# Far tokens of a fused transformer block transposed by VectorE from 32-blocks, and six weight sums issued in the MLP

## The chip, the cores and the metric

The kernel runs on one core of a Trainium2 chip. The metric is the device time of one execution in microseconds (us): 1777.04, the median of 3 runs (1775.67 to 1777.31). A core has TensorE (PE in the profile; PEld is its weight load), VectorE (DVE), ScalarE (ACT), GpSimd (POOL) and SyncE (SP, which here issues nearly all DMAs). Each engine takes its own instructions in the order in which the program lists them, and waits on semaphores where it needs another's result.

## The reference

All in float32: x is 2048 x 1024, wqkv 1024 x 3072, 32 heads of 32 features, an MLP of width 3584.

```python
qkv = layernorm(x) @ wqkv                       # split into q, k, v by head
pq, pk = (per head: q @ w_phi, k @ w_phi)
phi_q = [softmax(pq), softmax(-pq)];  phi_k = [softmax(pk), softmax(-pk)]
kv = einsum("hsf,hsd->hfd", phi_k, v);  z = sum over s of phi_k
o = (phi_q @ kv) / (phi_q . z + 1e-6)
h = x + o @ wo
out = h + relu(layernorm(h) @ w1) @ w2
```

## The kernel before

The 2048 tokens are 16 tiles of 128: tiles 0 to 7 are the near half, 8 to 15 the far half. Every product is done with both operands split into a high part (rounded to the fast format fp32r) and a low part (the rest), as three matmuls: high x high, high x low, low x high. A weight unit of 128 x 512 is loaded into a "raw" tile (6 of them), ACT makes the high part (L126), VectorE or GpSimd the low part (L131), into a ring of ten "w" tiles; the raw tile is then free for the next load.

Stages, in PE's order: for the near half the keys and values (four slabs s of 256 columns, one item for each tile and slab), then the queries (two slabs); the same for the far half; then the attention output and wo; then the MLP: 98 up items for each half of the tokens, and the down items. The MLP's two products are done in the manner of Strassen with seven products in place of eight, so it reads, beside blocks of w1 and w2, sums of blocks. These 56 weight sums are made ahead of time: `t_load` brings four blocks of 128 x 256 into one tile, `t_sum` subtracts four times on GpSimd (L401), `t_store` writes the tile to a scratch tensor t. `sums_at` says at which step each one stands: 45 before and in the attention stage, 11 in the MLP. In the MLP the tile is y2 (name "y" in the trace), with one buffer, so a load waits for the store before it.

The order of everything beside the matmuls is written out by hand. `when(step, f, ...)` hangs f on a step; a step is three large matmuls of PE. An item of the attention stage has 8 steps, an up item of the MLP 4. `up0` is the first step of the MLP. `W.advance` puts the loads and splits of weights between the steps, as the rings come free.

A tile of x is loaded (`ln_load`, L239), its mean and variance taken (`ln_stats`, `ln_power`, which leaves scale and bias), normalized by ACT (`ln_norm`, L262), transposed by PE in two groups of four (`ln_turn`, L281) into a PSUM bank "tp" (2 of them), from where ACT takes the high part (L180) and VectorE the low part (L181) into xT. xT has eight buffers, so far tile t can be written only when PE is done with near tile t - 8, in the second query slab. The statistics of the far tiles are taken much earlier, from a load of its own ("s", steps 80 to 214), and kept in scx; the far tile is loaded a second time. The far half's hidden states later go another way (`far_pair`): loaded so that VectorE's 32 x 32 transposes suffice, with scales spread over the partitions by `far_scale` (16 small matmuls, L833, and one ACT copy).

A chunk k of xT holds 128 features; before, features 128k to 128k + 127. The key and query weights are multiplied by w_phi beforehand ("folded"): slab 0 at the very start by `fold_mm` (L315), the others by `fold_all` (L326) at seven steps up to 232.

```python
turn = 8 * n + 1                                     # n: the item after near tile t - 8's last
load_ = turn - 88 + 8 * (t - HT) if t < HT + 4 else turn - 36
stages = (load_, None, None, turn - 8, turn + 1, turn + 1)
```

For the second half of the tokens in the MLP, its transposed states hT are loaded (L885, fourteen loads of 512 KB) at steps up0 + 344 to up0 + 407, each when the first half's last product of that kind is done, split by ACT (L893) and VectorE (L897), and read from step up0 + 392 on.

Of the kernel before, what the change touches and what calls it, by code (L numbers as in the profile page):

```python
# [46 lines left out]
UP = (1, 5, 6, 2, 7, 3, 4)  # L47
DOWN = (1, 5, 6, 3, 7, 2, 4)
OPENS = (1, 5, 2)
FOLD_STEPS = 31, 76, 104, 144, 176, 206, 232  # L50
BANK_OF = {6: 1, 7: 1, 4: 1, 3: 5}

# [90 lines left out]
def kernel(  # L143
# [31 lines left out]
    def f32(ap):  # L175
        return ap.bitcast(F32)
# [57 lines left out]
    def ln_load(key, parts):  # L234
        xin[key] = xlp.tile([P, D], F32, name="xl") if key[0] == "x" and key[1] >= HT and key[1] % 4 > 1 else \
            lnp.tile([P, D], F32, name="xin")
        n = D // len(parts)
        for j, p in enumerate(parts):
            sp.dma_start(xin[key][:, j * n:(j + 1) * n], p)  # L239
# [17 lines left out]
        xst[key] = sc  # L257

    def ln_norm(key):
        sc, src = xst.pop(("s", key[1]) if key[0] == "x" and key[1] >= HT else key), xin.pop(key)  # L260
        xnt[key] = src if key[0] == "h" else fp_ln.tile([P, D], F32, name="xn")
        act.activation(xnt[key], src, AF.Identity, bias=sc[:, 1:2], scale=sc[:, 0:1])  # L262

    def ln_norm_by(key, engines):

        sc, src = xst.pop(key), xin.pop(key)
        xnt[key] = xn = fp_ln.tile([P, D], F32, name="xn")
        n = D // len(engines)
        for j, eng in enumerate(engines):
            cols = slice(j * n, (j + 1) * n)  # L270
            if eng is act:
                act.activation(xn[:, cols], src[:, cols], AF.Identity, bias=sc[:, 1:2], scale=sc[:, 0:1])
            else:
                eng.tensor_scalar(xn[:, cols], src[:, cols], sc[:, 0:1], sc[:, 1:2], op0=ALU.mult, op1=ALU.add)

    def ln_turn(key, j, dst=None):

# [33 lines left out]
            wt_of[p, i] = t  # L311

    def fold_mm(k, ps, i):
        if True:
            pe.matmul(ps[:, i * P:(i + 1) * P], wt_of[0, i][:, k * P:(k + 1) * P],  # L315
                      bd[:, i, :], start=True, stop=True)

    def fold_all(p):

        banks = [(ac_bank if p == 1 else tp_bank)() for _ in range(2)] + [mm_bank() for _ in range(2)]  # L320
        for i in range(2):
            wt = wt_of.pop((p, i)).rearrange("p (c q d) -> p c q d", q=4, d=32)
            for r in range(4):
                rows = slice(32 * r, 32 * (r + 1))
                for q in range(4):
                    pe.matmul(banks[r][32 * q:32 * (q + 1), 256 * i:256 * (i + 1)],  # L326
                              wphi[rows, (2 * p + i) % 8, :], wt[rows, :, q, :], start=True, stop=True)
        fold_ps[p] = banks
# [26 lines left out]
    def load(key, t):  # L355

        kind = key[0]
        if kind == "kv":
            _, hf, s, k = key
            sp.dma_start(t[:, 0:256], wpk[s][k])  # L360
            sp.dma_start(t[:, 256:512], wv[s, k])
        elif kind == "q":
            _, _, s, k = key
            sp.dma_start(t, wpq[s][k])
        elif kind == "wo":
            _, hf, c = key
            sp.dma_start(t, wo[hf, c])
        elif kind == "a":
            sp.dma_start(t, ad[key[1:]])
        else:  # L370
            _, _, m, p = key
            w = 1 if kind == "w1" else 2
            sp.dma_start(t, block(w, p, *{1: (0, 0), 2: (1, 0), 3: (1, 1)}[m]) if m < 4
                         else td[w, p][:, {5: 0, 7: 3 - w, 4: w, 6: 3}[m], :])

    def block(w, p, r, c):

# [30 lines left out]
    def first_values():  # L408

        for k in range(0, NK, 2):  # L410
            if k == 4:
                ln_load(("x", 1), x_part(1))
            place = W.raws.take()
            t = place[1]
            sp.dma_start(t.rearrange("p (k f) -> p k f", k=2), wv[0, k:k + 2].rearrange("k p f -> p k f"))
            for i in range(2):
                first_raw[k + i] = t[:, 256 * i:256 * (i + 1)], place
        W.loaded = W.done = NK

# [407 lines left out]
    hst = {}  # L827

    def far_scale():
        ps = tp_bank()[:, 0:64].rearrange("p (g n s) -> p g n s", g=4, n=HT)  # L830
        for g in range(4):
            for a in range(4):
                pe.matmul(ps[32 * a:32 * (a + 1), g], ident.rearrange("p (t g) -> p g t", g=4)[:, g],  # L833
                          scx[:, :, 0, :], start=True, stop=True)
        act.activation(scx.rearrange("p n g s -> p g n s"), ps, AF.Copy)

# [236 lines left out]
    def when(step, f, *args):  # L1073
# [3 lines left out]
        else:  # L1077
# [200 lines left out]
    for b in range(2):  # L1278
# [7 lines left out]

    sixth, fourth = (10, 19, 28, 37, 46, 55), (10, 19, 28, 37)
    sums_at = [30, 39, 47] + [64 * i + k for i in (1, 2, 3) for k in sixth] + \
        [266, 276, 286, 296, 332, 342, 352, 362, 372] + \
        [64 * i + k for i, places in ((6, fourth), (7, fourth), (8, fourth), (9, (14, 26, 38))) for k in places] + \  # L1290
        [up0 + 424 + 30 * i for i in range(11)]
    for n, (w, p, j) in enumerate((w, p, j) for w in (1, 2) for p in range(NP) for j in range(2)):
        step = sums_at[n]
        half_on = sums_at.index(64 * 6 + 10)
# [122 lines left out]
```

## Time and profile before

| what | value |
|---|---|
| median of 3 runs | 1777.04 us |
| the profiled execution, whole | 1776.94 us |
| its span, first to last instruction | 1774.9 us |
| HBM traffic | 295.31 MB read, 137.89 MB written, 244 GB/s over the span |
| sums on GpSimd, tiles b, y, xn | 121.2, 38.4 and 22.5 us busy |

The span is cut into 40 slices on the page; a digit is the busy share in tenths:

```profile
DVE  7888778777789878664656664454434333343333
ACT  5322245333333342455555654444444444444442
POOL 4788745878847998432433344434354454544443
DMA  7899788655476777987889988787787777877775
```

A slice is 44.4 us. The far tiles stand in slices 5 and 6 (222 to 311 us), the MLP from slice 17 on. A group row of the profile names line, engine, operation, tiles and count, then "busy us, mean ns of one", then idle time of the engine before it and what ended that. A row of waits reads "who waited <- for whom: us in total, times, longest".

### The profile page before, as it was taken

What the parts mean: (1) busy time and instruction counts of PE and PEld (TensorE: products, weight loads), DVE (VectorE), ACT (ScalarE), POOL (GpSimd) and SP (SyncE); (2) the same over time, 40 slices, a digit from 0 to 9 for tenths busy, and PEclk for the clock granted to TensorE, in tenths of its full rate; (3) what the DMA queues carried; (4) which work ended last, traced back from release to release, by engine and by line L of the source; (5) the groups of instructions that cost most, each with busy time, mean ns of one, the idle gap of its engine ahead of it and who ended that gap; (6) DMA issues with size and microseconds to landing.
All of it is one profiled execution on the core that took longest, in us unless ns stands there. A gap on an engine that the chain in (4) does not pass through costs nothing.

```text
span 1774.9 us, 28930 instructions
## 1 busy us (share of the span) xinstructions
PE 1767.2 (100%) x10088; PEld 1528.4 (86%) x10088; DVE 1078.5 (61%) x1650; ACT 766.9 (43%) x1378; POOL 978.8 (55%) x990
## 2 busy tenths in 40 slices
PE   9999999999999999999999999999999999999999
PEld 8888888888888888888888888888888888888887
DVE  7888778777789878664656664454434333343333
ACT  5322245333333342455555654444444444444442
POOL 4788745878847998432433344434354454544443
PEclk9999999999999999999999999999999999999999
DMA  7899788655476777987889988787787777877775
GB/s 224 270 312 314 256 274 278 196 174 166 144 214 215 244 251 226 304 271 227 254 267 281 367 289 259 252 272 255 231 247 222 230 230 240 260 226 228 228 227 183
DMA packets 335234, 435.13 MB, mean 245 GB/s; under 512 B 29296, under 2 KB 195184, under 8 KB 335088
## 3 DMA queue, kind: packets, MB, share of 16 engines
q1 hardware_dynamic: 301008, 415.98, 73.8%
q10 hardware_dynamic: 34080, 17.31, 3.4%
q8 instruction: 79, 1.29, 0.3%
q14 instruction: 67, 0.55, 0.1%
HBM read 295.31 MB, written 137.89 MB: 244 GB/s over the span
## 4 chain that ended last, share of the span: by engine, by line
PE 92%; DVE 3%; DMA 2%; POOL 2%; issue 1%; ACT 0%; SPq 0%; ACTq 0%; DVEq 0%; POOLq 0%
PE mm L205 22%; PE mm L206 22%; PE mm L207 22%; PE ac L206 4%; PE ac L205 4%; PE ac L207 4%; PE tp L207 2%; PE tp L206 2%; PE tp L205 2%; PE mm L200 1%; PE mm L197 1%; PE mm L196 1%; PE tp L281 1%; PE ac L503 1%; POOL w L131 1%
## 5 line engine op out<-in xcount | busy, mean ns | idle before, releaser
L131 POOL TENSOR_TENSOR w<-raw,w 128x512 fp32r<-128x512 f32 x356 | 472.9, 1330 | 606.7 <-ACT w L126 582.6
L126 ACT ACTIVATE w<-raw 128x512 fp32r<-128x512 f32 x686 | 410.2, 625 | 482.7 <-PE mm L207 221.3
L131 DVE TENSOR_TENSOR w<-raw,w 128x512 fp32r<-128x512 f32 x330 | 273.7, 831 | 467.5 <-ACT w L126 461.5
L205 PE MATMUL mm<-w,xT 128*128 128x512 f32 x680 | 262.6, 386 | 0.0
L206 PE MATMUL mm<-w,xT 128*128 128x512 f32 x680 | 258.3, 380 | 0.4 <-POOL sc L254 0.4
L207 PE MATMUL mm<-w,xT 128*128 128x512 f32 x680 | 258.0, 379 | 0.0
L207 PE MATMUL mm<-hT,w 128*128 128x512 f32 x624 | 236.7, 379 | 0.0
L205 PE MATMUL mm<-hT,w 128*128 128x512 f32 x624 | 236.7, 379 | 0.0
L206 PE MATMUL mm<-hT,w 128*128 128x512 f32 x624 | 236.7, 379 | 0.0
L207 PE MATMUL mm<-w 128*128 128x512 f32 x392 | 148.7, 379 | 0.0
L205 PE MATMUL mm<-w 128*128 128x512 f32 x392 | 148.7, 379 | 0.0
L206 PE MATMUL mm<-w 128*128 128x512 f32 x392 | 148.7, 379 | 0.0
L205 PEld LDWEIGHTS mm<-w,xT 128*128 128x128 f32 x680 | 128.7, 189 | 22.2 <-issue 4.1
L401 POOL TENSOR_TENSOR b<-b 128x256 f32<-128x256 f32 x152 | 121.2, 797 | 47.7 <-DMA b<-in_w_dram 40.3
L206 PEld LDWEIGHTS mm<-w,xT 128*128 128x128 f32 x680 | 128.8, 189 | 18.4 <-POOL sc L254 0.9
L207 PEld LDWEIGHTS mm<-w,xT 128*128 128x128 f32 x680 | 128.8, 189 | 18.1 <-DVE xT L181 0.2
L206 PEld LDWEIGHTS mm<-hT,w 128*128 128x128 f32 x624 | 118.2, 189 | 16.6
L205 PEld LDWEIGHTS mm<-hT,w 128*128 128x128 f32 x624 | 118.2, 189 | 16.5
L207 PEld LDWEIGHTS mm<-hT,w 128*128 128x128 f32 x624 | 118.2, 189 | 16.5
L492 POOL TENSOR_TENSOR zacc<-zacc,kphi 128x512 f32<-128x512 f32 x60 | 79.2, 1320 | 16.0 <-DVE kphi L484 15.4
L476 ACT ACTIVATE ke<-ke 128x512 f32<-128x512 f32 x64 | 40.3, 630 | 100.9 <-DVE ke L472 100.8
L207 PEld LDWEIGHTS mm<-w 128*128 128x128 f32 x392 | 74.2, 189 | 10.4
(194 smaller groups left out, 3366.1 us busy)
## 6 DMA issues: line engine op xcount, KB each, us to landing
raw<-t SPq DMA_DIRECT2D x224, 256.0 KB, 4.1
raw<-ad SPq DMA_DIRECT2D x196, 256.0 KB, 3.1
raw<-in_w_dram SPq DMA_DIRECT2D x168, 256.0 KB, 3.5
ad<-c SPq DMA_DIRECT2D x112, 256.0 KB, 4.5
ad<-s SPq DMA_DIRECT2D x84, 256.0 KB, 4.7
b<-in_w_dram SPq DMA_DIRECT2D x38, 512.0 KB, 5.6
t<-b SPq DMA_DIRECT2D x38, 512.0 KB, 4.8
ed<-qe ACTq DMA_DIRECT2D x64, 256.0 KB, 3.7
```

Source lines behind the costliest of these rows:

```text
L126: nc.scalar.activation(w[:, 0, :], raw[1], AF.Copy)
L131: eng.tensor_tensor(out=w[:, 1, :], in0=raw[1], in1=w[:, 0, :].bitcast(F32), op=ALU.subtract)
L196: pe.matmul(ps, a_hi, woven(b_hi), start=first and k == 0, stop=False, skip_group_check=more)
L197: pe.matmul(ps, a_lo, woven(b_hi), start=False, stop=False, skip_group_check=more)
L200: pe.matmul(ps, a_hi, woven(b_lo), start=False, stop=last and j == n - 1, skip_group_check=more)
L205: pe.matmul(ps, a_hi, b_hi, start=first, stop=False, skip_group_check=more)
L206: pe.matmul(ps, a_hi, b_lo, start=False, stop=False, skip_group_check=more)
L207: pe.matmul(ps, a_lo, b_hi, start=False, stop=last, skip_group_check=more)
L281: pe.transpose(pt[:, k, :], xn[:, (4 * j + k) * P:(4 * j + k + 1) * P], ident)
L401: pool.tensor_tensor(out=tsum[*u, *out], in0=tsum[*u, *a], in1=tsum[*u, *b], op=ALU.subtract)
L476: act.activation(e_of[key], e_of[key], AF.Exp)
L492: pool.tensor_tensor(out=zacc[s], in0=zacc[s], in1=phi_of[key], op=ALU.add)
```

## The change

1. *Far tiles.* `ln_load` reads a far tile in four DMAs of 32 tokens: partition 32a + t holds token 32g + t's features 256a to 256a + 255, g by columns. Each partition has thus four tokens, so `x_scale` (step 226) spreads the scales as `far_scale` does. `x_norm` normalizes in place with four ACT instructions of 256 columns, `x_turn` transposes all 32 x 32 blocks with one VectorE instruction, `x_high` makes the high part on ACT, `x_low` the low part on GpSimd in two instructions. Tile t's transpose stands at step 334 + 11(t - 8), its load 26 steps ahead, its low part 6 steps behind.
2. *Features.* The blocks come out with four groups of 32 features in a chunk: chunk k holds features 256a + 32k + i. All that meets xT follows: near tiles are normalized into that order (`chunked`, `dst_order`), value rows are read in it (`value_rows`), and both folds take their columns in it. `fold_mm` becomes four matmuls with 32 output rows in place of one with 128; the first value loads are eight DMAs in place of four.
3. *Sums.* Five sums at steps 332 to 372 and one of four around 394 to 421 leave the attention stage. The MLP has 17 in place of 11, every 23 steps from up0 + 360 in place of every 30 from up0 + 424; their loads stand 12 steps ahead of the sum in place of 15.

```diff
+        if key[0] == "x" and key[1] >= HT:
+            for g in range(4):
+                sp.dma_start(xin[key][:, 256 * g:256 * (g + 1)], parts[0][32 * g:32 * (g + 1)].rearrange("t (a f) -> a t f", a=4))
+            return
...
-        act.activation(xnt[key], src, AF.Identity, bias=sc[:, 1:2], scale=sc[:, 0:1])
+        if key[0] == "x":
+            dst, src = chunked(dst), dst_order(src)
+        act.activation(dst, src, AF.Identity, bias=sc[:, 1:2], scale=sc[:, 0:1])
+    def chunked(xn):
+        return xn.rearrange("p (k a i) -> p a k i", k=NK, a=4)
+    def dst_order(x):
+        return x.rearrange("p (a k i) -> p a k i", k=NK, a=4)
+    def x_scale():
+        spread("p (g t) -> p g t")
+    def x_norm(t):
+        for g in range(4):
+            piece, sc = xin["x", t][:, 256 * g:256 * (g + 1)], scx[:, t - HT, g]
+            act.activation(piece, piece, AF.Identity, bias=sc[:, 1:2], scale=sc[:, 0:1])
+    def x_turn(t):
+        xnt["x", t] = xn = fp_ln.tile([P, D], F32, name="xn")
+        v.transpose(xn.rearrange("p (k g t) -> p g k t", g=4, k=NK), xin.pop(("x", t)).rearrange("p (g k i) -> p g k i", g=4, k=NK))
+    def x_high(t):
+        act.activation(xT[t][:, 0].rearrange("p k n -> p (k n)"), xnt["x", t], AF.Copy)
+    def x_low(t):
+        hi, lo = (xT[t][:, s].rearrange("p k n -> p (k n)") for s in range(2))
+        for j in range(2):
+            cols = slice(512 * j, 512 * (j + 1))
+            pool.tensor_tensor(out=lo[:, cols], in0=xnt["x", t][:, cols], in1=f32(hi[:, cols]), op=ALU.subtract)
...
     def fold_mm(k, ps, i):
-            pe.matmul(ps[:, i * P:(i + 1) * P], wt_of[0, i][:, k * P:(k + 1) * P],
-                      bd[:, i, :], start=True, stop=True)
+        for q in range(4):
+            cols = slice(256 * q + 32 * k, 256 * q + 32 * (k + 1))
+            pe.matmul(ps[32 * q:32 * (q + 1), i * P:(i + 1) * P], wt_of[0, i][:, cols], bd[:, i, :], start=True, stop=True)
...
+    when(226, x_scale)
...
-            load_ = turn - 88 + 8 * (t - HT) if t < HT + 4 else turn - 36
-            stages = (load_, None, None, turn - 8, turn + 1, turn + 1)
+            turn = FAR_X + FAR_X_EVERY * (t - HT)
+            for step, f, *args in ((-26, ln_load, ("x", t), x_part(t)), (-9, x_norm, t), (0, x_open, t), (0, x_turn, t),
+                                   (3, x_high, t), (6, x_low, t)):
+                when(turn + step, f, *args)
...
-        [266, 276, 286, 296, 332, 342, 352, 362, 372] + \
-        [64 * i + k for i, places in ((6, fourth), (7, fourth), (8, fourth), (9, (14, 26, 38))) for k in places] + \
-        [up0 + 424 + 30 * i for i in range(11)]
+        [266, 276, 286, 296] + \
+        [394, 406, 418] + [64 * i + k for i, places in ((7, fourth), (8, fourth), (9, (14, 26, 38))) for k in places] + \
+        [up0 + 360 + 23 * i for i in range(17)]
...
-        when(step - (7 if 256 < step < 400 else 15), t_load, w, p, j, home)
+        when(step - (7 if 256 < step < 430 else 12 if step > up0 else 15), t_load, w, p, j, home)
```

Three places in the order of instructions. First PE at the start of the program, from the warm-up matmuls (on ones) to the first large matmul; bd is w_phi on a block diagonal, wt the weights to be folded. Before:

```order
L1333 MATMUL tp<-ones 128x128 x16
L315 MATMUL ac<-bd,wt 128x128 x4
L281 MATMUL tp<-ident,xn 128x128 x8
L315 MATMUL ac<-bd,wt 128x128 x4
L315 MATMUL mm<-bd,wt 128x128 x8
L205 MATMUL mm<-w,xT 128x512
```

and with the change:

```order
L1383 MATMUL tp<-ones 128x128 x16
L353 MATMUL ac<-bd,wt 32x128 x16
L318 MATMUL tp<-ident,xn 128x128 x8
L353 MATMUL ac<-bd,wt 32x128 x16
L353 MATMUL mm<-bd,wt 32x128 x32
L206 MATMUL mm<-w,xT 128x512
```

Each of the 16 calls of the fold is now four, with 32 output rows; nothing else moved there. The eight rows "L281 MATMUL tp<-ident,xn 128x128 x8" of the far tiles further on are gone without a row in their place.

Second, GpSimd in the last items of the near queries and the first far keys (b is the tile of a weight sum, smq a small product of the queries' softmax, zacc the sum of phi_k). Before:

```order
L609 TENSOR_TENSOR smq<-qsm 128x16 x2
L401 TENSOR_TENSOR b<-b 128x256 x4
L609 TENSOR_TENSOR smq<-qsm 128x16 x2
L401 TENSOR_TENSOR b<-b 128x256 x4
L609 TENSOR_TENSOR smq<-qsm 128x16 x2
L401 TENSOR_TENSOR b<-b 128x256 x3
L609 TENSOR_TENSOR smq<-qsm 128x16 x2
L401 TENSOR_TENSOR b<-b 128x256 x2
```

and with the change, from the same place to the first accumulations of zacc:

```order
L132 TENSOR_TENSOR w<-raw,w 128x512
L298 TENSOR_TENSOR xT<-xn,xT 128x512 x2
L650 TENSOR_TENSOR smq<-qsm 128x16 x2
L132 TENSOR_TENSOR w<-raw,w 128x512
L442 TENSOR_TENSOR b<-b 128x256
L298 TENSOR_TENSOR xT<-xn,xT 128x512 x2
L650 TENSOR_TENSOR smq<-qsm 128x16 x2
L442 TENSOR_TENSOR b<-b 128x256 x3
L533 TENSOR_TENSOR zacc_360<-zacc_360,kphi 128x512
L650 TENSOR_TENSOR smq<-qsm 128x16 x2
L298 TENSOR_TENSOR xT<-xn,xT 128x512 x2
L442 TENSOR_TENSOR b<-b 128x256 x4
```

The far tiles' low parts stand where five sums stood, and the last three of them now share the queue with the sums and accumulations that follow.

Third, SP in the MLP between a store of the tile y and the load that follows it (ad are stores of the hidden layer, raw loads of weights). Before, the first such place:

```order
L404 DMA t_8_336<-y_11301 512x1x256
L941 DMA ad_4_0_300<-c_11276 128x512
L373 DMA raw<-in_w_dram 128x512
L941 DMA ad_4_1_301<-c_11296 128x512
L373 DMA raw<-t_2_316 128x512
L941 DMA ad_2_0_258<-c_11320 128x512
L391 DMA y_11466<-in_w_dram 128x4x256
```

and with the change, the first such place, which stands where the second half's hT is loaded:

```order
L930 DMA hT_8494<-hs_6_113 128x4x256
L445 DMA t_5_333<-y_10947 512x1x256
L930 DMA hT_8494<-hs_6_113 128x4x256
L986 DMA ad_1_12_130<-c_10901 128x512
L410 DMA raw<-t_1_315 128x512
L986 DMA ad_1_13_131<-c_10924 128x512
L432 DMA y_11069<-in_w_dram 128x4x256
L410 DMA raw<-in_w_dram 128x512
L930 DMA hT_8495<-hs_2_114 128x4x256
```

The store and the load are nearer to each other, and loads of hT stand around and behind them.

More of the change, by code (lines that the diff above doesn't have):

```diff
@@ L49 @@
 OPENS = (1, 5, 2)
+FAR_X, FAR_X_EVERY = 334, 11
 FOLD_STEPS = 31, 76, 104, 144, 176, 206, 232
@@ L259, in ln_norm @@
     def ln_norm(key):
-        sc, src = xst.pop(("s", key[1]) if key[0] == "x" and key[1] >= HT else key), xin.pop(key)
-        xnt[key] = src if key[0] == "h" else fp_ln.tile([P, D], F32, name="xn")
-        act.activation(xnt[key], src, AF.Identity, bias=sc[:, 1:2], scale=sc[:, 0:1])
+        sc, src = xst.pop(key), xin.pop(key)
+        xnt[key] = dst = src if key[0] == "h" else fp_ln.tile([P, D], F32, name="xn")
+        if key[0] == "x":
[21 more added lines that the diff above has]
+            pool.tensor_tensor(out=lo[:, cols], in0=xnt["x", t][:, cols], in1=f32(hi[:, cols]), op=ALU.subtract)
+        del xnt["x", t]
     def ln_norm_by(key, engines):
@@ L267, in ln_norm_by @@
         xnt[key] = xn = fp_ln.tile([P, D], F32, name="xn")
-        n = D // len(engines)
+        n = NK // len(engines)
         for j, eng in enumerate(engines):
-            cols = slice(j * n, (j + 1) * n)
+            dst, x_ = (f(t)[:, :, j * n:(j + 1) * n] for f, t in ((chunked, xn), (dst_order, src)))
             if eng is act:
-                act.activation(xn[:, cols], src[:, cols], AF.Identity, bias=sc[:, 1:2], scale=sc[:, 0:1])
+                act.activation(dst, x_, AF.Identity, bias=sc[:, 1:2], scale=sc[:, 0:1])
             else:
-                eng.tensor_scalar(xn[:, cols], src[:, cols], sc[:, 0:1], sc[:, 1:2], op0=ALU.mult, op1=ALU.add)
+                eng.tensor_scalar(dst, x_, sc[:, 0:1], sc[:, 1:2], op0=ALU.mult, op1=ALU.add)
     def ln_turn(key, j, dst=None):
@@ L321, in fold_all @@
         for i in range(2):
-            wt = wt_of.pop((p, i)).rearrange("p (c q d) -> p c q d", q=4, d=32)
+            wt = wt_of.pop((p, i)).rearrange("p (q c d) -> p c q d", q=4, d=32)
             for r in range(4):
@@ L360, in load @@
             sp.dma_start(t[:, 0:256], wpk[s][k])
-            sp.dma_start(t[:, 256:512], wv[s, k])
+            sp.dma_start(t[:, 256:512], value_rows(s)[:, :, k])
         elif kind == "q":
@@ L374, in load, with value_rows @@
                          else td[w, p][:, {5: 0, 7: 3 - w, 4: w, 6: 3}[m], :])
+    def value_rows(s):
+        return wv[s].rearrange("k p f -> (k p) f").rearrange("(a k i) f -> a i k f", a=4, k=NK)
     def block(w, p, r, c):
@@ L414, in first_values @@
             t = place[1]
-            sp.dma_start(t.rearrange("p (k f) -> p k f", k=2), wv[0, k:k + 2].rearrange("k p f -> p k f"))
             for i in range(2):
+                sp.dma_start(t[:, 256 * i:256 * (i + 1)], value_rows(0)[:, :, k + i])
                 first_raw[k + i] = t[:, 256 * i:256 * (i + 1)], place
@@ L829, in far_scale, with spread @@
     def far_scale():
+        spread("p (t g) -> p g t")
+    def spread(order):
         ps = tp_bank()[:, 0:64].rearrange("p (g n s) -> p g n s", g=4, n=HT)
@@ L832, in far_scale @@
             for a in range(4):
-                pe.matmul(ps[32 * a:32 * (a + 1), g], ident.rearrange("p (t g) -> p g t", g=4)[:, g],
+                pe.matmul(ps[32 * a:32 * (a + 1), g], ident.rearrange(order, g=4)[:, g],
                           scx[:, :, 0, :], start=True, stop=True)
```

5 lines of the change are left out of this document (3 added, 2 removed).

## The prediction, made before the changed kernel was run

> **What bounds the kernel now.** I read the page first: busy times, clock, chain of waits.
>
> ```profile
> span 1774.9 us, 28930 instructions
> PE 1767.2 (100%) x10088; PEld 1528.4 (86%) x10088; DVE 1078.5 (61%) x1650; ACT 766.9 (43%) x1378; POOL 978.8 (55%) x990
> ...
> PEclk9999999999999999999999999999999999999999
> ...
> PE 92%; DVE 3%; DMA 2%; POOL 2%; issue 1%; ACT 0%; SPq 0%; ACTq 0%; DVEq 0%; POOLq 0%
> ```
>
> TensorE (PE) is busy from end to end at the full clock, and 92% of the chain that ended last is PE. A busy PE can still hide short waits, so the second view is what PE waited for, over the whole run:
>
> ```profile
> PE tp L1333 <- POOL ones L1329: 1.6, 1, 1.6
> PE tp L281 <- DVE xn L274: 0.7, 1, 0.7
> PE mm L200 <- POOL w L131: 0.6, 1, 0.6
> PE mm L206 <- POOL sc L254: 0.4, 1, 0.4
> ```
>
> That is 3.3 us in all. So a microsecond of PE work taken out is a microsecond of the end, as long as nobody else becomes late; and work on any other engine is free until PE has to wait for it. The profiled execution took 1776.94 us (span 1774.9 and 2.0 around it), 0.1 below the median 1777.04; the sum below is made against 1776.94.
>
> **The term that pays: eight groups of transposes.** The third view is PE's timeline around the first transposes of a far tile (start, duration), and from the chain of waits in order of time the first and the last of the eight groups.
>
> ```profile
> 257.39 0.38 PE L207 MATMUL mm<-w,xT 128*128 128x512 f32 x1
> 257.61 1.04 PE L281 MATMUL tp<-ident,xn 128*128 128x128 f32 x8
> 258.40 0.46 PE L205 MATMUL mm<-w,xT 128*128 128x512 f32 x1
> 258.70 0.38 PE L206 MATMUL mm<-w,xT 128*128 128x512 f32 x1
> ...
> 257.77 0.87 PE tp L281 x8
> ...
> 299.51 0.87 PE tp L281 x8
> ```
>
> Matmuls of one stream start 0.216 us apart (257.39, 257.61 for the next in line). Across the group two starts are 258.70 - 257.39 = 1.31 apart where 0.43 would do: **0.88 us per tile**, including the slower first matmul behind it. Eight such groups stand between 257.8 and 299.5, one for each of tiles 8 to 15, and the order shows none of them in the change: **-7.0 us**.
>
> **What PE gets instead.** The new scale spreading at step 226 is the same code as one that stands already at the start of the MLP, 16 matmuls of 16 columns (32 records):
>
> ```profile
> 770.98 0.38 PE L197 MATMUL ac<-hT,w 128*128 128x512 f32 x1
> 771.29 0.68 PE L833 MATMUL tp<-scx,ident 128*32 128x16 f32 x32
> 771.90 0.48 PE L196 MATMUL ac<-hT,w 128*128 128x512 f32 x1
> 772.22 0.38 PE L197 MATMUL ac<-hT,w 128*128 128x512 f32 x1
> ...
> L326 PE MATMUL tp<-wt,wphi x192: 373/374/399, 73.8 to 190.2; 32*32 32x256 f32 x192
> ...
> 181.13 0.27 POOL L256 TENSOR_SCALAR scx<-mv,scx 128x1 f32<-128x1 f32 x1
> ```
>
> 772.22 - 770.98 = 1.24 against 0.43: **+0.8 us**. It adds a wait, for the last of the scales, which GpSimd ends at 181.4. The last weight fold is issued at step 232, six steps later, and its last records start at 190.2; less 1.6 for the fold and 6 x 0.65 for the steps, PE reaches the spreading near 184.7, 3.3 us after the scales. Behind it on PE is everything, so any lateness beyond 3.3 us would cost in full.
>
> At the start the fold's 16 calls become 64 with 32 output rows each, four of them in the four column groups.
>
> ```profile
> 10.77 1.95 PE L315 MATMUL mm<-bd,wt 128*128 128x128 f32 x16
> 12.48 0.46 PE L205 MATMUL mm<-w,xT 128*128 128x512 f32 x1
> ...
> 522.74 0.38 PE L200 MATMUL mm<-w,xT 128*128 128x512 f32 x1
> 523.05 1.09 PE L715 MATMUL ac<-qe,kvL 64*32 64x256 f32 x32
> 524.08 0.48 PE L196 MATMUL mm<-w,xT 128*128 128x512 f32 x1
> ```
>
> Now the last eight calls, 16 records, take 12.48 - 10.77 = 1.7 us, 0.11 each. If the four groups run one after the other, 128 records of 0.11 cost 14 us instead of 32 for 3.5: +10.5. If side by side, four cost what one does: 0. The nearest row is L715, which also writes to 32-row groups: 32 records of 256 columns in 524.08 - 523.05 = 1.03 us, 0.03 each, with twice the columns; that is side by side. I take 0 and keep up to +0.5. One rule of the Trainium skill, the page TensorEngine Tiling (Array Packing), section Key Properties, speaks against this edit: changing the tiling mode drains TensorE. The trace bears it out in size: from 522.74 to 523.05 is 0.31 instead of 0.216. By the row alone, 0.1 at each of four new switches is 0.4 us, of which the waits that PE has anyway before 20 us can swallow a part: **+0.2 us**, 0 to 0.4.
>
> The first two tiles' normalization now writes its output in pieces of 32. PE waits for VectorE's piece of it once (0.7 us, L274 above).
>
> ```profile
> 16.73 0.81 DVE L274 TENSOR_SCALAR xn<-xin,sc 128x1024 f32<-128x1024 f32 x1
> ...
> L181 DVE TENSOR_TENSOR xT<-tp,xT 128x512 fp32r<-128x512 f32 x16 | 10.3, 683 | 2.9 <-ACT xT L180 2.7
> ```
>
> No run shows the strided form. At the pace of L181 (0.68 for 512) it would take 1.3 us instead of 0.81, all of it on PE's wait: 0 to +0.5; I take 0, since only the order of equal pieces changes. By the Trainium skill, VectorE: DVE Perf Modes, section Mode 2×_2P, the fast mode asks for operands in SBUF and an even outermost dimension, and it is 4 here; by that the price is 0, which no run here shows. The four extra loads of values on SP (eight of half the size) go out while the first tiles are awaited and are used after 10 us; 0.
>
> Sum: -7.0 + 0.8 + 0.2 = **-6.0: 1770.9 us**.
>
> **What has to stay hidden in the attention stage.** These are the stage's sums (258 to 304 us: PE, PEld, DVE, ACT, POOL busy), the sums that leave it, and the operations nearest to the new ones.
>
> ```profile
> 258.00:304.00 46.00, 46.00 (x245) 40.86 (x244) 41.31 (x64) 28.29 (x39) 23.34 (x40) 1.00 0.93 291
> ...
> L401 POOL TENSOR_TENSOR b<-b 128x256 f32<-128x256 f32 x20 | 14.6, 731 | 18.9 <-DMA b<-in_w_dram 17.9
> ...
> L702 DVE STREAM_TRANSPOSE qe<-qe 128x1024 f32<-128x1024 f32 x32 | 39.4, 1231 | 13.5 <-POOL qe L696 11.6 <-POOL qe L691 1.9
> L131 POOL TENSOR_TENSOR w<-raw,w 128x512 fp32r<-128x512 f32 x356 | 472.9, 1330 | 606.7 <-ACT w L126 582.6 <-DVE c L929 7.9 <-DMA raw<-in_w_dram 7.8
> ...
> L838 DVE STREAM_TRANSPOSE y<-xin 128x1024 f32<-128x1024 f32 x4 | 11.7, 2914 | 3.7 <-DMA ad<-s 3.7
> ...
> 311.44 0.99 POOL L401 TENSOR_TENSOR b<-b 128x256 f32<-128x256 f32 x1 [3.64 <-DMA b<-in_w_dram]
> ```
>
> Without its seven groups this stretch lasts 46 - 6 = 40 us. VectorE: 41.3 less 10.3 (L181, low parts) plus five transposes (the tiles are 11 steps apart). A transpose is 1.23 us by L702 and 2.9 by L838, whose output goes to every fourth element; the new one writes runs of 32, so 1.23: 37 of 40 us; with 2.9 it would be 45.5. GpSimd: 23.3 less 14.6 for the sums plus five times two subtractions of 1.33: 22 us, and its 17.9 us of waiting for the sums' loads goes too. ACT has 12 us spare. So PE stays covered, narrowly on VectorE. Later GpSimd gets tight: tile 15's low part is issued at step 417 and PE reads it at 432, 9.7 us on; it takes 2.7, so GpSimd may be 7 us behind. Between steps 394 and 417 it has two sums (6.4), two accumulations (2.6), two low parts (5.3) and small ones, 15 us in 15, and one load wait of 3.6 as at 311.44: about 4 behind. Cost 0, with 3 us to go.
>
> **What has to stay hidden in the MLP.** Seventeen sums on one buffer, every 23 steps (14.9 us) instead of eleven every 30 (19.4). Load, four subtractions, store, then the next load: a closed ring. Its pieces, and the traffic where the first rounds now fall (before, the first load went out at 1024):
>
> ```profile
> L401 POOL TENSOR_TENSOR y<-y 128x256 f32<-128x256 f32 x44 | 38.4, 872 | 8.5 <-DMA y<-in_w_dram 4.4 <-issue 1.6
> ...
> y<-in_w_dram SPq DMA_DIRECT2D x11, 512.0 KB, 6.2
> t<-y SPq DMA_DIRECT2D x11, 512.0 KB, 4.1
> ...
> 985.00:1025.00 40.00, 40.00 (x187) 35.08 (x187) 28.60 (x31) 26.66 (x41) 12.56 (x8) 1.00 1.05 370
> ...
> y<-in_w_dram SPq DMA_DIRECT2D x1, 512.0 KB, 9.3
> ...
> L196 PE MATMUL mm<-hT,w x24: 379/379/380, 1009.0 to 1041.4; 128*128 128x512 f32 x24
> L885 SPq DMA_DIRECT2D hT<-hs x14: 529/530/698, 984.7 to 1022.2; - x14
> ```
>
> 6.2 + 3.5 + 4.1 and some 0.5 of issue is 14.3 us, just under the period of 14.9. But the second half's first product (step up0+392) starts at 1009.0, so the first load, 44 steps earlier, falls at 980.5, and rounds one to three into a stretch where the DMA engines are full (share 1.05, 370 GB/s) with the fourteen hT loads; there a load took 9.3. A store then makes SP wait for late subtractions, the next load makes SP wait for the store, and behind both on SP stand hT loads and raw weights. I make the first three rounds 18 to 19 us, so SP ends about 8 us later than now. What covers that: the last hT load goes out at 1022.2, lands in about 7.2, needs some 3 us of splitting, and PE wants it at step up0+440, 1009.0 + 48 x 0.65 = 1040.1: 7.7 us to spare. I count 0, at the edge.
>
> **Rivals.** (1) *The full stretch breaks the cover*: SP is not 8 but 10 to 13 us late, hT or a raw tile comes late, PE waits 2 to 5 us once: 1773 to 1776, say 1774. For it: the 9.3 and the share of 1.05; against: PE did not wait there with SP already 6.8 us behind its step (first hT load at 984.7, step time 977.9). (2) *VectorE or GpSimd is late for the far tiles* (the transpose nearer 2.9 than 1.23, or a longer load wait at step 394): 1 to 4 us, 1773. (3) *The ring of the y buffer becomes the bound, and the kernel slower*: with SP held in it, PE follows its pace. 17 rounds of c us against 17 of 14.9, less the 7.7 of cover: PE loses 17(c - 14.9) - 7.7; that eats the gain of 6.0 from c = 15.7 on, and at c = 16.2 it is 14.4 lost, 1785. Against: the medians give 14.3, and in quieter places a load takes less. (4) *A little more comes back*: the wait of 0.6 for a weight at step 325 goes with the freed queues, and the switches cost nothing: 1770.1. That the change doesn't do what it says is out: the order has no transposes there.
>
> **How the numbers follow.** Chances: forecast 0.58, rival 1 0.20, rival 2 0.08, rival 3 0.07, rival 4 0.07. A measurement here can tell about 0.2%, 3.6 us, so faster means below 1773.5: forecast, rival 4, a third of rival 1 and nearly none of rival 2: 0.72; within 0.2%: 0.22; slower, rival 3: 0.06. The range runs from 1769.2 (rival 4, no cost at the start) to 1775.8 (rivals 1 and 2 with nearly all of their span), leaving rival 3 out; the forecast's own is 1769.9 to 1772.3, the bounds of its start terms.
>
> **What would show it.** No group of eight at 257 to 300 on PE; the spreading near 185 with about 0.8 us; a transpose of about 1.23 us; no line of PE waiting for xT or hT; y loads on the ring 14.9 us apart. A wait of PE on hT or w between 1020 and 1045, or y rounds over 15.7 us, makes me wrong; so does a far tile's subtraction ending within a step of its first use.

## The result, and the profile after

| | us |
|---|---|
| before, median of 4 runs beside it (1775.67 to 1777.31) | 1776.53 |
| after, median of 4 runs (1839.42 to 1844.97) | 1844.30 |
| ratio, 95% interval | 1.0375 (1.0362 to 1.0388) |
| the profiled execution, whole; its span | 1844.73; 1842.9 |

The change costs 68 us. The page of the changed kernel, for the lines shown of before:

```profile
span 1842.9 us, 29112 instructions
PE 1783.1 (97%) x10152; PEld 1529.6 (83%) x10152; DVE 1092.1 (59%) x1642; ACT 771.1 (42%) x1395; POOL 1006.0 (55%) x1006
...
PE   8899898689999999999999989999999999999999
...
PEclk9899999789999999999999999999999999999999
DMA  6588774555557677788798998798887677877775
...
PE 69%; DMA 12%; DVE 7%; POOL 5%; issue 3%; SPq 2%; ACT 2%; ACTq 0%; DVEq 0%; POOLq 0%
```

PE now stops, and it does so in slices 0 to 8 (46 us a slice), the attention stage, and once in the MLP (slice 23). DMA has 12% of the chain where it had 2%. What PE waited for:

```profile
PE mm L197 <- ACT w L127: 15.5, 7, 6.7
PE mm L206 <- DVE qe L627: 8.8, 2, 7.2
PE ac L544 <- DVE kphi L525: 7.3, 3, 4.1
PE mm L201 <- POOL w L132: 5.1, 2, 3.3
PE mm L207 <- POOL sc L259: 4.9, 2, 3.6
PE mm L197 <- ACT hT L938: 3.8, 2, 2.2
```

These are splits of weights, softmaxes and scales: PE's suppliers are late, and the chain shows that it is not for their own work. The chain of waits in order of time (start, duration) names the loads, at three of the stops:

```profile
74.25 8.27 DMA raw<-in_wv_dram
...
293.76 9.26 DMA xin<-in_x_dram
...
303.51 8.43 DMA ed<-qe
...
316.45 10.02 DMA xin<-in_x_dram
```

The list of DMA issues of before has, as its last number, the median time in us from issue to landing of the same tiles:

```profile
ed<-qe ACTq DMA_DIRECT2D x64, 256.0 KB, 3.7
xin<-in_x_dram SPq DMA_DIRECT2D x19, 512.0 KB, 5.6
raw<-in_wv_dram SPq DMA_DIRECT2D x56, 128.0 KB, 3.4
```

On this chain a value load of 128 KB is on its way for 8.3 us, a far tile's load of 128 KB for 9 to 10, and `ed<-qe`, which the change doesn't touch, for 8.4. The chain picks out the late ones. The list of after gives no landing times for them; its trace has them in the semaphore updates (how they are counted stands with e1 below). The medians are 7.4 us for the value loads, where before has 3.4, and 8.8 for the far loads, where before's whole tile of 512 KB has 5.6. `ed<-qe` has 4.5, and before too had one of 8.6. The untouched loads that nearly doubled are `raw<-wpk`, 128 KB each: 6.4 and not 3.3. One stretch of both kernels, before first (busy us by engine, then clock, DMA share and GB/s):

```profile
300.00:350.00 50.00, 50.00 (x293) 43.69 (x292) 40.96 (x77) 16.45 (x30) 32.98 (x37) 1.00 0.73 222
```

```profile
300.00:350.00 50.00, 31.38 (x120) 25.26 (x119) 30.89 (x44) 22.62 (x36) 15.99 (x23) 0.80 0.44 138
```

Everybody works less, the DMA engines too: 138 GB/s at a share of 0.44. The loads are slow while the DMA engines stand idle for more than half of their time.

To see where the 68 us arise, the large matmuls, of which every variant has the same 7776 in the same order, are numbered in each trace, and the start of the n-th is set against before's. The near half's keys and values end with the 768th and its queries with the 1152nd. The 100th still stands in the first items, the 900th in the near queries ahead of the first far tile's load, the 1400th behind the far tiles' first products, the 4000th in the MLP ahead of the second half's products.

| large matmul | 1st | 100th | 900th | 1400th | 4000th | 7776th |
|---|---|---|---|---|---|---|
| before, us | 12.5 | 41.2 | 236.4 | 353.5 | 955.2 | 1770.2 |
| after | -0.1 | +6.2 | +31.1 | +58.8 | +60.0 | +67.7 |
| e1, before + rows in 4 groups | -0.5 | -0.5 | +23.5 | +26.1 | +27.2 | +27.2 |
| e3, after, far loads by 32 | +0.1 | +6.3 | +30.1 | +37.1 | +37.8 | +44.7 |
| e5, before + moved sums | 0.0 | 0.0 | +1.2 | +0.3 | +0.6 | +10.5 |
| e7, stride of 8 | +3.7 | +4.1 | +11.2 | +9.8 | +9.9 | +17.2 |
| e9, runs of 8 | +1.1 | +1.4 | +3.7 | -1.5 | +0.2 | +8.9 |
| e12, with later MLP sums, earlier loads | +1.0 | +1.1 | +2.8 | -3.7 | -2.9 | -2.7 |

Three blocks: 31 us in the near half, 28 net in the far half, 8 in the MLP. Of the 31, the first 6 arise by the 100th matmul, where after has its eight first value loads and e1 still has the old ones; of the other 25, e1 shows 24. Each row is one trace: e10, with the same near half as e9, has +7.1 at the 900th where e9 has +3.7, so differences of some 3 us there say little.

### The profile page after: what moved, and what is told of

The parts are those of the page before. It is cut to its first block, busy times and chain, and to the rows that moved or that the text cites. A ratio compares the mean times of both kernels' runs of the same rounds, so it can differ in the third digit from the quotient of the medians.

```text
span 1842.9 us, 29112 instructions
## 1 busy us (share of the span) xinstructions
PE 1783.1 (97%) x10152; PEld 1529.6 (83%) x10152; DVE 1092.1 (59%) x1642; ACT 771.1 (42%) x1395; POOL 1006.0 (55%) x1006
## 4 chain that ended last, share of the span: by engine, by line
PE 69%; DMA 12%; DVE 7%; POOL 5%; issue 3%; SPq 2%; ACT 2%; ACTq 0%; DVEq 0%; POOLq 0%
PE mm L206 16%; PE mm L207 16%; PE mm L208 16%; PE ac L206 3%; PE ac L208 3%; PE ac L207 3%; DMA xin<-in_x_dram 3%; DMA raw<-in_wv_dram 3%; PE tp L207 2%; PE tp L206 2%; PE tp L208 2%; POOL b L442 2%; DMA ed<-qe 2%; POOL w L132 1%; DMA b<-in_w_dram 1%
## 5 line engine op out<-in xcount | busy, mean ns | idle before, releaser
L132 POOL TENSOR_TENSOR w<-raw,w 128x512 fp32r<-128x512 f32 x356 | 479.4, 1351 | 486.3 <-ACT w L127 468.6
L132 DVE TENSOR_TENSOR w<-raw,w 128x512 fp32r<-128x512 f32 x330 | 281.3, 854 | 479.6 <-ACT w L127 472.6
L206 PE MATMUL mm<-w,xT 128*128 128x512 f32 x680 | 266.1, 391 | 9.5 <-DVE qe L627 8.8
L207 PE MATMUL mm<-w,xT 128*128 128x512 f32 x680 | 261.7, 385 | 4.9 <-POOL sc L259 4.9
L208 PE MATMUL mm<-w,xT 128*128 128x512 f32 x680 | 260.9, 384 | 0.0
L206 PEld LDWEIGHTS mm<-w,xT 128*128 128x128 f32 x680 | 130.7, 192 | 34.5 <-issue 14.7
L207 PEld LDWEIGHTS mm<-w,xT 128*128 128x128 f32 x680 | 131.0, 193 | 23.9 <-POOL sc L259 5.5
L208 PEld LDWEIGHTS mm<-w,xT 128*128 128x128 f32 x680 | 130.7, 192 | 19.2 <-DVE xT L182 0.2
L442 POOL TENSOR_TENSOR b<-b 128x256 f32<-128x256 f32 x136 | 107.6, 792 | 44.5 <-DMA b<-in_w_dram 37.9
L442 POOL TENSOR_TENSOR y<-y 128x256 f32<-128x256 f32 x68 | 58.6, 862 | 122.7 <-DMA y<-in_w_dram 110.5
```

Of the source, the lines that this page charges most:

```text
L132: eng.tensor_tensor(out=w[:, 1, :], in0=raw[1], in1=w[:, 0, :].bitcast(F32), op=ALU.subtract)
L206: pe.matmul(ps, a_hi, b_hi, start=first, stop=False, skip_group_check=more)
L207: pe.matmul(ps, a_hi, b_lo, start=False, stop=False, skip_group_check=more)
L208: pe.matmul(ps, a_lo, b_hi, start=False, stop=last, skip_group_check=more)
L442: pool.tensor_tensor(out=tsum[*u, *out], in0=tsum[*u, *a], in1=tsum[*u, *b], op=ALU.subtract)
```

## Experiments

**Is it the shape of the loads?** A value load of the change reads 128 rows of 1 KB as 4 groups of 32. That differs from before in two ways: the rows are scattered, and the slowest dimension of the transfer has 4 steps and not 128. Two kernels, both built on before, tell these apart.

```diff
 # e1: q = 4; e2: q = 16
-            sp.dma_start(t[:, 256:512], wv[s, k])
+            sp.dma_start(t[:, 256:512], wv[s].rearrange("k p f -> (k p) f").rearrange("(a k i) f -> a i k f", a=q, k=NK)[:, :, k])
```

> The kernel before, with the 56 value loads behind the first reading the rows by the change's pattern (4 groups of 32 rows, 1 KB a row, the same 128 rows' worth of bytes); x keeps its order of features, so the values are multiplied by the wrong rows of their weights (that part of the output is another). Nothing else is changed. Theory A (the shape: a transfer whose slowest dimension has 4 steps is carried by 4 of the 16 DMA engines, whatever it reads): these loads land in 6 to 9 us and not 3.4, the transfers beside them land later too, and the time is 1790 to 1815 us. Theory B (the scatter: 32-KB groups and not 128 KB in one piece are slow to read): the same here, 1790 to 1815. Theory C (the loads do not matter; the loss of the change is from the far tiles' new work on ScalarE, VectorE and GpSimd and from the moved sums): 1773 to 1780.

> As the run beside it, but 16 groups of 8 rows: the same 1 KB rows, scattered in smaller pieces still, with a slowest dimension of 16 steps (the values are again multiplied by other rows of their weights). Theory A (the shape): the loads land in 3 to 4 us and the time is 1773 to 1780 us. Theory B (the scatter): at least as slow as with 4 groups, 1790 to 1820. Theory C (the loads do not matter): 1773 to 1780.

e1: 1803.24 us, ratio 1.0154 (1.0131 to 1.0176). e2: 1778.67, ratio 1.0012 (1.0003 to 1.0021). The page's count of DMA packets, first of before, then of e1; that of e2 is before's to the last digit:

```profile
DMA packets 335234, 435.13 MB, mean 245 GB/s; under 512 B 29296, under 2 KB 195184, under 8 KB 335088
```

```profile
DMA packets 334562, 435.13 MB, mean 241 GB/s; under 512 B 28624, under 2 KB 194512, under 8 KB 334416
```

The same bytes, but e1 has 672 packets fewer, all of them small: 12 for each of its 56 loads. In before's trace 24,176 packets (and one odd one) have 4 bytes, which is 16 for each of its 1511 transfers: by that count the notice of its end from each of the 16 DMA engines. A load in 4 groups leaves 4 of them: it is served by 4 engines. One in 16 groups is served by all. The landing time of e2's loads is in its list of DMA issues; e1's chain of waits has two of its own:

```profile
raw<-in_wv_dram SPq DMA_DIRECT2D x56, 128.0 KB, 3.7
```

```profile
57.95 5.74 DMA raw<-in_wv_dram
...
66.89 8.23 DMA raw<-in_wv_dram
```

3.7 us with 16 engines, 5.7 and 8.2 for these two with 4. In the trace each of e1's 56 loads leaves 5 updates of its semaphore where every other transfer leaves 16; the last of them gives the landing, a median of 7.1 us (4.0 to 10.0). The untouched `raw<-wpk` beside them went from 3.3 to 6.2. The Trainium skill has this rule: in DMA: Bandwidth & Descriptors, section "Why a DMA increments its semaphore by 16 and not by 1", a transfer is cut over the largest number of engines up to 16 that divides the slowest dimension of both sides. Here that is 4 (of 4 and 128), and the twelve missing packets a load agree. Theory B, the scatter, falls with e2, which scatters in smaller pieces still and is 1.8 us slower than before (0.5 to 3.7 by its interval).

**The far loads.** In the change each is 32 tokens as 4 blocks of 256 features: 4 steps again. Cutting the tile by blocks, not by tokens, makes the slowest dimension 32, with the same count, size and runs:

```diff
-            for g in range(4):
-                sp.dma_start(xin[key][:, 256 * g:256 * (g + 1)], parts[0][32 * g:32 * (g + 1)].rearrange("t (a f) -> a t f", a=4))
+            for a in range(4):
+                sp.dma_start(xin[key][32 * a:32 * (a + 1)].rearrange("t (g f) -> t g f", g=4),
+                             parts[0][:, 256 * a:256 * (a + 1)].rearrange("(g t) f -> t g f", g=4))
```

> The changed kernel, with a far tile's four loads cut by the blocks of features and not by the blocks of tokens: again 4 loads of 128 KB in 1 KB runs to the same places, but the slowest dimension of each is 32 tokens and not 4 blocks. The result is the same. Theory A (the shape): the far loads land in 3 to 5 us and not 8 to 10, the stop at 310 to 345 us shrinks, and the time falls by 15 to 40 us to 1804 to 1829. Theory B (the scatter) and theory C (the far tiles' work on the engines): 1839 to 1849.

1822.5 us, 22 less than after. The packets of after, then of e3:

```profile
DMA packets 337604, 435.15 MB, mean 236 GB/s; under 512 B 28592, under 2 KB 198576, under 8 KB 337456
```

```profile
DMA packets 337988, 435.16 MB, mean 239 GB/s; under 512 B 28976, under 2 KB 198960, under 8 KB 337840
```

384 more, 12 for each of the 32 loads. The table puts the gain between the 900th and the 1400th matmul. The near half's loss is as in after: it is the values'. Between the 1152nd and the 1344th matmul e3 still loses 14 us where e9 loses 2; the value loads go on there, but e3 and e9 differ in more than their shape, and this part was not tried apart.

**Values in four plain loads.**

```diff
-            sp.dma_start(t[:, 256:512], value_rows(s)[:, :, k])
+            for a in range(4):
+                sp.dma_start(t[32 * a:32 * (a + 1), 256:512], value_rows(s)[a, :, k])
```

> The changed kernel, with each value load cut into 4 loads of 32 rows in one piece (the first loads for two chunks at a time): the same rows to the same places, 168 more loads to issue at about 0.55 us each on SP. The result is the same. Theory A (the shape): the stops before 200 us shrink, and the time falls by 20 to 40 us to 1804 to 1824, unless SP's extra 92 us of issue take it back. Theory B (the scatter; 32-KB pieces stay): 1839 to 1850. Theory C: 1839 to 1850.

1852.76 us: 8 more, not 20 to 40 less. The value loads of 32 KB land in 2.0 us (median, by the semaphore updates), so their shape is cured. But a weight's four loads take SP 1.8 us to issue, one after the other, and now the splits wait for SP, which has 4% of the chain (SPq) and not 2%; the parts of the chain (first line) and the longest wait:

```profile
PE 68%; DMA 9%; POOL 8%; DVE 6%; SPq 4%; issue 4%; ACT 1%; ACTq 0%; POOLq 0%; DVEq 0%
```

```profile
PE mm L197 <- ACT w L127: 23.7, 9, 14.3
```

Here more transfers were no cure for a transfer on few engines; what helped below is a pattern that SP issues once.

**The moved sums,** alone on before (e5), and put back in the changed kernel (e6). Both swap this table and the loads' distance:

```diff
-        [266, 276, 286, 296, 332, 342, 352, 362, 372] + \
-        [64 * i + k for i, places in ((6, fourth), ...
-        [up0 + 424 + 30 * i for i in range(11)]
+        [266, 276, 286, 296] + \
+        [394, 406, 418] + [64 * i + k for i, places in ((7, fourth), ...
+        [up0 + 360 + 23 * i for i in range(17)]
```

> The kernel before, with the moved weight sums alone: five sums of steps 332 to 372 and one of 394 to 421 go to the MLP, which has 17 sums every 23 steps and not 11 every 30. Theory A (of the change's 68 us, only the stop at 1090 to 1110 us, 7.7 us over the matmuls' own times, is the sums'; the rest is the shape of the loads): PE stops in the MLP alone, and the time is 1777 to 1786 us. Rival D (the denser sums are free in the MLP, and that stop came from elsewhere): 1773 to 1777. Rival E (the moved sums carry much of the loss, in the attention too): over 1790.

> The changed kernel with the sums put back to the places and load distances of before; the rest of the change stays. Theory A: the stops of the attention stay and that of the MLP goes: 1834 to 1841 us. Rival D (the MLP stop is not the sums'): 1842 to 1847. Rival F (the sums had to leave GpSimd, since five of them among the far tiles' low parts delay both): over 1848, with waits for GpSimd at 300 to 400 us.

e5: 1786.74 us, ratio 1.0057 (1.0042 to 1.0072), nearly all of it behind the 4000th matmul: theory A's place, 0.7 us above its range. Its waits and its chain:

```profile
PE mm L196 <- ACT hT L893: 3.2, 2, 2.1
```

```profile
1004.88 7.49 DMA t<-y
...
1037.32 8.81 DMA hT<-hs
```

A sum's store is on its way for 7.5 us, SP waits with the next sum's load, the hT loads stand behind it and themselves take 8.8 us. e6: 1857.6, 13 us slower than after: rival F. With five sums among the far tiles' low parts, PE's longest wait is for the far keys' features (us in total, times, longest), and the chain runs through GpSimd's sums, low parts and accumulations alone from 380 to 397 us:

```profile
PE ac L544 <- DVE kphi L525: 21.3, 4, 15.9
```

The 13 us are net: by the 1400th matmul e6 is at +79.6 where after is at +58.8, 21 us worse, and the MLP gives 8 back. In the attention stage the sums had to go; in the MLP their new places were too early.

**Other fours.** With chunk k holding the features 8q + k, a chunk's value rows have one stride, so a single load has 128 steps. The engines then read x and the fold weights at a stride of 8 elements.

```diff
-        return wv[s].rearrange("k p f -> (k p) f").rearrange("(a k i) f -> a i k f", a=4, k=NK)
+        return wv[s].rearrange("k p f -> (k p) f").rearrange("(q k) f -> q k f", k=NK)
...
-        v.transpose(..., xin.pop(("x", t)).rearrange("p (g k i) -> p g k i", g=4, k=NK))
+        v.transpose(..., xin.pop(("x", t)).rearrange("p (g i k) -> p g k i", g=4, k=NK))
...
-            wt = wt_of.pop((p, i)).rearrange("p (q c d) -> p c q d", q=4, d=32)
+            wt = wt_of.pop((p, i)).rearrange("p (q d c) -> p c q d", q=4, d=32)
```

> The changed kernel with other fours of features, so that every load has a slowest dimension of 32 or 128: chunk k holds the features 8 q + k, its value rows are then 128 rows at one stride of 8 KB (1 KB each, one load, and one load of 2 KB rows for two chunks at the start), the near tiles' normalization, VectorE's turn and the folds read at a stride of 8 elements, the first folds are one matmul again and not four, and a far tile's loads are cut by blocks of features as in e3. The moved sums stay. The result is the same. Theory A: the attention's stops go, the far tiles' transposes stay saved (7 us), and only the MLP stop of some 8 us is left: 1770 to 1783 us. Theory C (far tiles' work on the engines) and any price of the strided reads: over 1790.

> As e7, and the sums at the places of before. Theory A: without the MLP stop, before less the far transposes: 1766 to 1775 us, faster than both kernels. Rival F (sums among the far tiles' low parts delay both on GpSimd): slower than e7.

e7: 1796.27 us, 48 less than after, but above its 1783. The value loads land in 3.5 us, the far loads in 3.4 to 3.8 (medians of its page). The stride has a price, in groups of e7 (between the bars: busy us, mean ns of one):

```profile
L363 PE MATMUL mm<-wt,wphi 32*32 32x256 f32 x224 | 16.5, 628 | 0.0
L270 ACT ACTIVATE xn<-xin,sc 128x1024 f32<-128x1024 f32 x6 | 13.7, 2280 | 6.9 <-POOL sc L262 6.9
L290 DVE STREAM_TRANSPOSE xn<-xl 128x1024 f32<-128x1024 f32 x4 | 8.1, 2023 | 0.0
L352 PEld LDWEIGHTS mm<-bd,wt 128*128 128x128 f32 x16 | 3.9, 335 | 0.0
```

e8 was a miss: 1810.94, 15 us slower than e7 and not faster (+35.4 at the 1400th matmul where e7 has +9.8), with one long wait for a weight's low part on GpSimd; rival F again:

```profile
PE mm L201 <- POOL w L132: 10.0, 1, 10.0
```

**Runs of 8,** the shape of e2: chunk k holds 64o + 8k + j. The reads change as above, with `"(o k j) f -> o j k f"` for the rows; the first folds' weights are copied into chunks once.

> e7 with other fours again: chunk k holds the features 64 o + 8 k + j (o 0 to 15, j 0 to 7), so that a value load has 16 groups of 8 rows (the shape of e2) and the engines read runs of 8 elements and not single elements at a stride; the weights of the first folds are put into chunks once by VectorE and GpSimd (128x512 each, twice), and VectorE's turn is 4 instructions of 128x256. The result is the same. Theory G (e7's 10 us of loss in the attention are the stride of 8 elements: its fold matmuls took 628 ns and not 384, its weight loads 332 and not 192, the near tiles' normalization 2280 and not 1244, the turn 2.02 us and not 1.21): these fall back to near the old values and the time is 1783 to 1790 us. Rival H (runs of 8 are no faster than a stride, or the loss is from the far tiles' work itself): 1793 to 1800.

1784.29 us, as theory G said. The same operations in e9 (the turn is now 4 of 128x256):

```profile
L373 PE MATMUL mm<-wt,wphi 32*32 32x256 f32 x224 | 9.9, 385 | 0.0
L270 ACT ACTIVATE xn<-xin,sc 128x1024 f32<-128x1024 f32 x6 | 7.5, 1248 | 6.5 <-POOL sc L262 6.5
L292 DVE STREAM_TRANSPOSE xn<-xl 128x256 f32<-128x256 f32 x16 | 5.5, 404 | 0.0
L355 PEld LDWEIGHTS mm<-bd,b 128*128 128x128 f32 x16 | 1.9, 192 | 0.0
```

**The MLP's sums, begun later,** in e9 and in before:

```diff
-        [up0 + 360 + 23 * i for i in range(17)]
+        [up0 + 424 + 25 * i for i in range(17)]
-        when(step - (... 12 if step > up0 else 15), t_load, w, p, j, home)
+        when(step - (... 15), t_load, w, p, j, home)
```

> e9 with the MLP's 17 sums every 25 steps from the place where before had its first one (up0 + 424), loads 15 steps ahead as before. Theory I (the MLP stop is from the sums' loads and stores that fall on the transfers of 1000 to 1050 us, at the start of the second batch half, and not from the number of sums): the stop goes, 7 us less than e9, 1772 to 1783 us. Rival J (17 sums are too many wherever they start): within 3 us of e9, with stops in the MLP.

> The kernel before with the moved sums as in e10 (17 in the MLP every 25 steps from up0 + 424), beside e5 where they began at up0 + 360 every 23. Theory I: 1774 to 1779 us, the 10.7 us of e5 gone. Rival J: over 1782.

e10: 1779.0 us, ratio to before 1.0009 (0.9999 to 1.0019); e11: 1777.44, 1.0001 (0.9992 to 1.0011). Theory I: seventeen sums cost nothing there, if the first falls behind the hT loads; in e11 its load goes out at 1024.9 us, the last hT load at 1022.9. The period (25 for 23) and the loads' lead (15 steps for 12) were changed with the start. The period hardly matters: e9, with 23, loses nothing more behind that stop (+8.9 at the 4500th matmul and at the last). The lead was not tried apart.

**The last microseconds.** e10 with the first folds' weights copied in four pieces, and `sums_at = [28, 37, 47]` for `[30, 39, 47]`.

> e10 with two edits aimed at what its trace still shows against before (1.1 us at the first large matmul, 4.6 us more by 91 us): the first folds' weights are put into chunks in four pieces per tile and not two, so that the first fold waits for a shorter copy; and the first two weight sums stand 2 steps earlier, since SP, which issues in order, waited for the sum of step 30 at 51 to 56 us with the next eight chunks' loads behind its store. If these two are what is left: 1771 to 1776 us, a little faster than before. If the later start of the first fold alone holds the loads back (SP's store was not in the way): 1776 to 1780, as e10.

1776.47 us, ratio 0.9999 (0.999 to 1.0008): at the edge of its two cases, and no faster than before. Its profiled execution took 1774.57 with the last large matmul 2.7 us ahead of before's, but its eleven runs spread from 1773.3 to 1778.9. No version that is measurably faster than before was found.

## Why the prediction was wrong

- **The step that failed** is the one that priced the new loads: "The four extra loads of values on SP (eight of half the size) go out while the first tiles are awaited and are used after 10 us; 0." These eight alone cost 6 us by the 100th matmul (after +6.2 and e3 +6.3, both from about 0 at the 1st; e9, with eight loads served by 16 engines, goes from +1.1 to +1.4). In after's chain one of them and the tile of x behind it are each on their way for 9 us:

```profile
5.22 8.93 DMA raw<-in_wv_dram
14.15 9.49 DMA xin<-in_x_dram
```

  The 56 value loads behind them and the 32 far loads got no term at all. They were taken for the old ones, since bytes and runs are about the same; the shape was not looked at. e1 shows 26 us for the 56 value loads, e3 22 us for the far loads, and e9, whose largest difference from after is that every load is served by 16 engines, is back to before by the 1400th matmul. None of the rivals had this mechanism; the one slower rival, with 0.06, had another place.
- **The MLP:** "I count 0, at the edge". Mechanism right (rival 1: store, next load, hT loads behind both on SP), size wrong: 7.7 us in after and 9.9 alone (e5, from the 4000th matmul on), not 0, and not rival 1's 2 to 5. The mis-sized term is SP's lateness. In e5 the last hT load goes out at 1037.9 us, in before at 1022.2: 15.7 later and not 8, against the cover of 7.7. The first round of the ring took 24 us where 18 to 19 were forecast: its store alone took 7.5 where the ring had 4.1 for it. The cover was short too: the hT load of the chain took 8.8 where 7.2 stood, and before's own last one had taken 8.9.
- **The transposes, -7.0: right.** From the 900th to the 1200th large matmul e12 gains 7.9 us on before (+2.8 to -5.1), which is 7.0 and the 0.8 of a stop that before had at 254 us (rival 4's term). In e3 the same step shows even beside the slow value loads, 7.0 from the 900th to the 1152nd; in after 5.3 show up to the 1100th, and then the next stop buries it.
- **The small terms** held. The first fold, one normalization and the spreading in the changed kernel's timeline (start, duration):

```profile
10.53 1.93 PE L353 MATMUL mm<-bd,wt 128*32 128x128 f32 x64
12.39 0.48 PE L206 MATMUL mm<-w,xT 128*128 128x512 f32 x1
...
20.69 0.80 DVE L311 TENSOR_SCALAR xn<-xin,sc 128x1024 f32<-128x1024 f32 x1
...
215.58 0.38 PE L208 MATMUL mm<-w,xT 128*128 128x512 f32 x1
215.89 0.45 PE L878 MATMUL tp<-scx,ident 128*32 128x16 f32 x32
216.27 0.48 PE L206 MATMUL mm<-w,xT 128*128 128x512 f32 x1
```

  The first fold in four column groups ends as before (12.39 against 12.48): side by side, 0. The spreading costs 0.69 - 0.22 = 0.5 (0.8 forecast) and waits for nothing, here and in e12, where it stands at 187.6 us, near the forecast 185. The normalization into pieces of 32 takes 0.80 (0.81).
- **The cover in the attention** held where the loads were in time: the turn takes 1.21 us (1.23 forecast), a low part 1.36 (1.33). And the sums did have to leave: e6 and e8 lose 13 and 15 us net with them back.

Why the repaired change (e12) still ties with before is open in part. Its one trace has 1.0 us lost at the start, where the first folds wait for the copy of their weights, some 2 more by the 900th matmul, 7.9 gained at the transposes, and 2.4 given back later; that leaves it 2.7 ahead, where the median of its runs is level with before's. The 2 us by the 900th are within what e9 and e10 differ by there, and their cause was not tried apart.

## What to carry to other kernels

When an edit changes how a transfer walks its memory, look at the count of its slowest dimension on both sides, not only at bytes and run length: 4 steps cost 128-KB loads a median of 7.1 to 8.8 us here, where 16 or more cost 3.4 to 4.8, and untouched loads of the same size beside them went from 3.3 to over 6. The sign on a page is a low DMA share beside late loads, and a drop in small packets, here by 12 a transfer. The same data could be cut the other way at no cost in e3, and in e9 the layout was chosen so that the walk has many steps.

## What the runs showed of the hardware

- A read of float32 at a stride of 8 elements took 2.02 us and not 1.21 for VectorE's 128x1024 transpose, 2.28 and not 1.25 for ScalarE's 128x1024, 628 ns and not 385 for a matmul's 256 moving columns, 335 and not 192 for a weight load of 128 columns. Runs of 8 elements were at full pace: 385 ns and 1.25 us in e9, and 404 ns for a transpose of 128x256, which lies on one line with before's 674 ns for 128x512 and 1.21 us for after's 128x1024. For the weight load they were not tried, since e9 loads copied weights.
- A stop of PE can cost more than its length. Behind the stop at 78 to 82 us the chain has starts 0.43 us apart, not 0.22:

```profile
86.24 0.43 PE mm L206
86.66 0.43 PE mm L207
87.09 0.43 PE mm L208
```

  and the granted clock over 74 to 90 us is 0.68 (the number ahead of the DMA share and the GB/s):

```profile
74.00:90.00 16.00, 10.79 (x32) 7.32 (x30) 7.87 (x17) 4.95 (x9) 5.86 (x6) 0.68 0.52 142
```

  After's large matmuls have 61 such distances, before's none: 61 by 0.216 is 13 us of the 68. Not every stop does it: behind the 1.3 us that PE waited for scales at 24 us the starts were 0.22 apart again.
